# Attention softmax of a fused kernel: mask by a TensorE product, one maximum and one subtraction per group, other order of the first loads

## The chip, the cores and the metric

The kernel runs on one core of a Trainium2 chip. The metric is device time in microseconds for one execution, as a median of repeated runs. A profiled execution is a single one of them, with a trace of every instruction. TensorE is called PE here (its weight loads PEld), VectorE is DVE, ScalarE is ACT, GpSimd is POOL, and SP is the engine whose queue issues the DMA transfers.

## The reference

```python
def _attn_ref(q, k, v):                       # 2 batches, 8 heads, 768 positions, head size 64
    k_sum = k.reshape(B, H, nb, 32, D).max(axis=3)
    v_sum = v.reshape(B, H, nb, 32, D).mean(axis=3)
    scores_l = scale * q @ k.T                # kept where |i - j| < 16, else -1e9
    scores_s = scale * q @ k_sum.T + log(32)
    a = softmax of [scores_l, scores_s], with 1e-9 added to the sum
    return a @ concatenate([v, v_sum])
def reference(...):
    x = attention, as 1536 tokens x 512
    x = (h * cos(h)) @ w_out,  h = x @ w_in           # 512 -> 2048 -> 512
    return layernorm(h * softmax(h)) * g_ln @ w_out2, h = x @ w_in2   # 512 -> 1024 -> 512
```

## The kernel before

Attention takes the first quarter of the time and the two feed-forward layers the rest. Heads go in 8 **pairs** (two heads on 128 partitions), each pair in 3 **groups** of 4 tiles of 64 queries, so there are 24 groups. A loop of 29 **steps** (lines 592 to 658) is a software pipeline: in step s, PE makes the scores of group s+1 (`emit_s`, tile `sps`, one of two PSUM banks), DVE and POOL take mask and maximum of group s (`emit_max`), ACT exponentiates group s-1 (`emit_exp`), DVE sums group s-2 and POOL normalises it (`emit_sum`, `emit_norm`), PE transposes group s-4 (`emit_t`) and multiplies group s-5 by v (`emit_av`). A group's scores are 128 x 480: 4 tiles with a window of 96 keys and 24 block maxima each.

Each pair also has to be prepared. The loads of k and q (`load_heads`, two buffers each) are laid side by side by a copy (`pair_k` on DVE, `pair_q` on ACT, tiles `kg` and `qg`, one buffer each), and PE transposes them in the step after the copies (`emit_k`, `emit_q`); three pairs are in flight. The means of v over blocks come from a second load of v, `vb`, once for each batch: `sum_v` (one DVE reduction for one head of each pair, five POOL additions for the other), `scale_v` on ACT, and `place_vsum`, a DMA that writes them under the window of v in `vt` (three buffers). `sum_v(0)` stands in step 1 and `sum_v(1)` in step 8; the load for the second, `load_vb(1)`, is issued in step 5, into the one `vb` buffer.

The order on every engine is the order in which the code is written: nothing reorders it, and an instruction that waits holds up all behind it in its queue, SP's DMA issues too. PE's row also holds `warm_up` products (two or three in each step before step 15) and from step 15 on the first 48 products `h` of the first feed-forward layer (`FILL`). Between steps 9 and 20 the first weights are converted (`rebias` on ACT, `finish` on DVE, `split` on ACT and POOL), and in steps 7, 10, 13 and 16 a quarter of the attention's output is split into two parts (`split_x`, tile `xs`, ACT and then POOL).

The softmax of one group is, before: four DVE instructions that add the mask from SBUF and take the maximum (line 500), a POOL subtraction (503), the exponential (508), a DVE sum (512), a DVE addition of 1e-9 to the 128x4 sums (516, `emit_guard`), after other DVE work its reciprocal (520), and a POOL product (521).

Of the kernel before, what the change touches and what calls it, by code (L numbers as in the profile page):

```python
# [19 lines left out]
QT = 64  # L20
# [13 lines left out]
def fused_kernel(  # L34
# [56 lines left out]
    wide = w_in.dtype == mybir.dt.int64  # L91
    LOWEST = -3.0e38
    WSTEPS = (9, 10, 12, 13, 15, 17, 18, 19)
# [3 lines left out]
    DVE_X = 19  # L97
    DVE_NORM = 99
    LAST = 5
# [234 lines left out]
    def attention():  # L334
        st = ExitStack()
        with st:
            io = st.enter_context(tc.tile_pool(name="io", bufs=2))
            fix = st.enter_context(tc.tile_pool(name="fix", bufs=1))
            sm_p = st.enter_context(tc.tile_pool(name="sm", bufs=6))

            NM = NG + 2
            mask = fix.tile([P, NM, KW], F32, name="mask")

            q_t, k_t, v_t, kx_t, vs_t, qk_t, ks_t = {}, {}, {}, {}, {}, {}, {}
# [15 lines left out]

            def side_by_side(t, name, scalar):
# [3 lines left out]
                if scalar:  # L365
                    nc.scalar.activation(out=to, in_=t, func=AF.Copy)
                else:
                    nc.vector.tensor_copy(to, t)
                return o

            def pair_k(n):
                k_t[n] = side_by_side(k_t[n], "kg", False)

            def pair_q(n):
                q_t[n] = side_by_side(q_t[n], "qg", True)

# [116 lines left out]

            def emit_max(G):
                g = G % GPP
                sm = sm_p.tile([P, NG, KW], F32, tag="sm", name="sm")
# [8 lines left out]
                sm_t[G] = sm  # L505

            def emit_exp(G):
                nc.scalar.activation(out=sm_t[G], in_=sm_t[G], func=AF.Exp)  # L508

            def emit_sum(G):  # L510
                ss = sm_p.tile([P, NG], F32, tag="ss", name="ss")
                nc.vector.tensor_reduce(out=ss, in_=sm_t[G], op=ALU.add, axis=AX.X)
                sum_t[G] = ss

            def emit_guard(G):
                nc.vector.tensor_scalar_add(sum_t[G], sum_t[G], 1e-9)

            def emit_norm(G):
                sm, ss = sm_t[G], sum_t.pop(G)
                nc.vector.reciprocal(out=ss, in_=ss)  # L520
                (nc.vector if G >= DVE_NORM else nc.gpsimd).tensor_tensor(  # L521
                    out=sm, in0=sm, in1=ss.unsqueeze(2).to_broadcast([P, NG, KW]), op=ALU.mult)

            def emit_t(G):
                sm = sm_t.pop(G)
                aps = bank(2, "aps").rearrange("p (i s) -> p i s", i=NG)[0:KW]
                for i in range(NG):
                    nc.tensor.transpose(aps[:, i, :], sm[:, i, :], ident)
                at_t[G] = aps
# [50 lines left out]
            emit_q(0)  # L580
            emit_kx(0)
            emit_qx(0)
            warm_up(3)
# [8 lines left out]
            for step in range(NGR + LA):  # L592
# [27 lines left out]
                if LT <= step < NGR + LT:  # L620
                    emit_at(step - LT)
                if summed:
                    emit_guard(step - LN)
                weights.finish()
# [297 lines left out]
```

## Time and profile before

| | |
|---|---|
| median of 3 runs | 517.97 us (517.88 to 519.25) |
| the profiled execution | 516.67 us, its span 514.6 us |
| PE busy | 489.6 us, 95% of the span |
| DVE, ACT, POOL busy | 60%, 54%, 30% |
| attention ends, first product `y` of the feed-forward | 117.26 us |

From 117 us on PE is never without work, and none of that part is touched by the change. What the change can give or cost lies in the first 117 us. A line of a timeline gives start, duration, engine, source line and tiles, and in brackets how long the engine stood idle before and what ended that.

### The profile page before, as it was taken

Reading aid. Unit: us, or ns where it says so; the run is one execution under the profiler, and the core shown is the slowest. Engines: PE = TensorE matmul, PEld = TensorE weight load, DVE = VectorE, ACT = ScalarE, POOL = GpSimd, SP = SyncE. Lnnn points to the kernel's source line nnn. Section 1 sums busy time; section 2 is a strip of 40 time slices with the busy share of each in tenths; the row PEclk is TensorE's granted clock in tenths of the full one; section 3 lists DMA queues with packets and bytes.
Section 4 is the critical chain, followed back from the end, with each engine's and each line's share of the span. In section 5 each row is a group of like instructions: output and inputs, shape, how many; then the busy total and the mean of one; then the engine's idle time right before and its main releaser. Section 6 shows DMA issues by size and latency. Waiting matters only on the chain.

```text
span 514.6 us, 7653 instructions
## 1 busy us (share of the span) xinstructions
PE 489.6 (95%) x2855; PEld 395.2 (77%) x2863; DVE 309.7 (60%) x684; ACT 275.4 (54%) x504; POOL 155.9 (30%) x147
## 2 busy tenths in 40 slices
PE   7589798899999999999999999999999999999997
PEld 4366576667888888888888888888887888888887
DVE  2586878786444447466565654646577755665561
ACT  3356798775768666565565653787422223222221
POOL 0477888742422222232232220244103102110000
PEclk8979899999999999999999999999999999999999
DMA  8799995600132322322323321220000000000001
GB/s 250 181 225 194 259 256 141 181 2 1 55 110 82 110 95 82 123 82 91 114 83 97 108 82 41 83 82 2 0 1 21 22 20 22 20 20 22 37 26 41
DMA packets 44516, 44.57 MB, mean 87 GB/s; under 512 B 21440, under 2 KB 36416, under 8 KB 44096
## 3 DMA queue, kind: packets, MB, share of 16 engines
q1 hardware_dynamic: 44480, 44.09, 29.5%
q8 instruction: 22, 0.36, 0.3%
q14 instruction: 14, 0.11, 0.1%
HBM read 39.76 MB, written 3.15 MB: 83 GB/s over the span
## 4 chain that ended last, share of the span: by engine, by line
PE 75%; DVE 6%; DMA 5%; ACT 5%; POOL 4%; SPq 3%; issue 2%; POOLq 0%; DVEq 0%; ACTq 0%
PE y L275 25%; PE h L233 23%; PE o L799 12%; PE h L721 11%; DMA vb<-in_v_dram 4%; PE tp L769 2%; POOL vb L409 1%; POOL sm L521 1%; POOL sm L503 1%; DMA qt<-in_q_dram 1%; SPq L397 1%; DVE vm L405 1%; PE sps L489 1%; POOL w L186 1%; ACT sm L508 1%
## 5 line engine op out<-in xcount | busy, mean ns | idle before, releaser
L233 PE MATMUL h<-xs,w 128*128 128x512 f32 x576 | 141.5, 392 | 1.2 <-ACT qx L475 1.2
L275 PE MATMUL y<-gs,w 128*128 128x512 f32 x576 | 138.2, 389 | 0.0
L275 PEld LDWEIGHTS y<-gs,w 128*128 128x128 f32 x576 | 108.0, 188 | 22.5
L233 PEld LDWEIGHTS h<-xs,w 128*128 128x128 f32 x576 | 107.1, 188 | 23.6 <-ACT qx L475 1.3
L186 POOL TENSOR_TENSOR w<-s,w 128x512 fp32r<-128x512 f32 x48 | 62.1, 1295 | 161.3 <-ACT w L185 139.8
L242 ACT ACTIVATE r<-h 128x512 int32<-128x512 f32 x48 | 28.7, 598 | 86.0 <-PE h L233 86.0
L247 DVE SCALAR_TENSOR_TENSOR r<-r,h 128x512 f32<-128x512 int32 x48 | 32.9, 686 | 67.2 <-ACT r L242 67.0
L799 PE MATMUL o<-w,ls 128*128 128x512 f32 (+1 forms) x312 | 67.8, 374 | 1.4 <-DVE ls L773 1.4
L721 PE MATMUL h<-w,xs 128*128 128x512 f32 x288 | 68.7, 393 | 0.0
L170 DVE SCALAR_TENSOR_TENSOR s<-raw 128x512 int32<-128x512 int32 x48 | 36.4, 757 | 48.3 <-ACT raw L163 40.9
L799 PEld LDWEIGHTS o<-w,ls 128*128 128x128 f32 x312 | 55.3, 188 | 12.2 <-DVE ls L773 1.9
L721 PEld LDWEIGHTS h<-w,xs 128*128 128x128 f32 x288 | 53.3, 188 | 10.7
L738 ACT ACTIVATE e<-h,st 128x1024 f32<-128x1024 f32 (+1 forms) x13 | 13.6, 1050 | 64.3 <-DVE st L734 60.8
L756 POOL TENSOR_TENSOR st<-st,mhalf 128x1 f32<-128x1 f32 x12 | 6.6, 552 | 118.1 <-DVE st L755 105.9
L489 PE MATMUL sps<-kx,qx 64*64 64x120 f32 x384 | 27.5, 288 | 12.1 <-DVE mx L500 12.0
L489 PEld LDWEIGHTS sps<-kx,qx 64*64 64x64 f32 x384 | 21.6, 144 | 22.7 <-DVE mx L500 14.8
L203 POOL TENSOR_TENSOR xs<-X,xs 128x512 fp32r<-128x512 f32 x22 | 28.8, 1314 | 30.7 <-ACT xs L202 30.7
L252 ACT ACTIVATE r<-r,half_pi 128x512 f32<-128x512 f32 x48 | 34.5, 718 | 1.3 <-DVE r L247 1.3
L263 DVE TENSOR_TENSOR gs<-h,gs 128x512 fp32r<-128x512 f32 x48 | 32.6, 679 | 4.1 <-ACT gs L262 3.9
L257 DVE TENSOR_TENSOR h<-h,r 128x512 f32<-128x512 f32 x48 | 32.9, 685 | 0.4 <-ACT r L252 0.4
L162 ACT ACTIVATE raw<-raw 128x512 f32<-128x512 f32 x48 | 32.0, 666 | 0.0
L163 ACT ACTIVATE raw<-raw 128x512 int32<-128x512 uint32 x48 | 31.9, 666 | 0.0
(73 smaller groups left out, 564.3 us busy)
## 6 DMA issues: line engine op xcount, KB each, us to landing
raw<-in_moe_w_in_dram SPq DMA_DIRECT2D x24, 512.0 KB, 3.5
raw<-in_moe_w_out_dram SPq DMA_DIRECT2D x24, 512.0 KB, 3.8
vt<-in_v_dram SPq DMA_DIRECT2D x16, 240.0 KB, 6.4
kt<-in_k_dram SPq DMA_DIRECT2D x8, 384.0 KB, 7.9
qt<-in_q_dram SPq DMA_DIRECT2D x8, 384.0 KB, 6.6
vb<-in_v_dram SPq DMA_DIRECT2D x8, 384.0 KB
out_dram<-osb SPq DMA_DIRECT2D x11, 256.0 KB, 2.0
vt<-vm SPq DMA_DIRECT2D x8, 144.0 KB
```

The lines of the kernel that those rows point to most:

```text
L162: nc.scalar.activation(out=hw, in_=hw, func=AF.Prelu, scale=REBIAS, alpha=NEGATIVE)
L170: nc.vector.scalar_tensor_tensor(out=self.f32[i], in0=t[:, :, 1], scalar=3, in1=t[:, :, 0], op0=ALU.logical_shift_left, op1=ALU.bitwise_or)
L186: nc.gpsimd.tensor_tensor(out=w[:, 1, :], in0=f, in1=as32(w[:, 0, :]), op=ALU.subtract)
L233: nc.tensor.matmul(h, lhsT=w[:, a, f * P:(f + 1) * P], rhs=xs_of[tb, c][:, b_, :], start=(m == 0), stop=(m == 3 * KC - 1))
L247: nc.vector.scalar_tensor_tensor(out=r, in0=r.bitcast(I32), scalar=TWO_PI, in1=h_of[step], op0=ALU.mult, op1=ALU.subtract)
L252: nc.scalar.activation(out=r, in_=r, func=AF.Sin, scale=-1.0, bias=half_pi)
L257: nc.vector.tensor_tensor(out=h, in0=h, in1=r, op=ALU.mult)
L263: nc.vector.tensor_tensor(out=gs[:, 1, :], in0=r, in1=as32(gs[:, 0, :]), op=ALU.subtract)
L275: nc.tensor.matmul(y[e], lhsT=w[:, a, e * P:(e + 1) * P], rhs=gs[:, b_, :], start=(f == 0 and i == 0), stop=(f == GF - 1 and i == 2))
L489: nc.tensor.matmul(sps[h, i, :], lhsT=qx[h, t * QT:(t + 1) * QT], rhs=kx[h, t, :], start=True, stop=True)
L721: nc.tensor.matmul(banks[n], lhsT=xs_of[NTB + t // TPB, c][:, a, t0:t0 + P], rhs=weights.done[w2i[c][n]][:, b_, :], start=(m == 0), stop=( ...
L799: nc.tensor.matmul(o, lhsT=ls_of[t][f // 4][:, a, s0:s0 + P], rhs=w[:, b_, cols], start=(f == 0 and i == 0), stop=(f == NF2 - 1 and i == 2))
```

## The change

- **Mask.** A product of `twice` (the identity plus itself shifted by 64 rows, 128x128) and `maskr` (128x480 of the mask, its upper half rounded, its lower half the remainder) starts each group's PSUM bank; the scores are accumulated on it. `make_mask` builds both tiles once, with two DVE instructions and one on ACT.
- **Maximum.** One DVE reduction over the bank, negated, and one DVE addition of it from PSUM into `sm` replace the four DVE instructions and the POOL subtraction.
- **Guard.** The six `sm` buffers have a 121st column that holds 1e-9, so the sum includes it; `emit_guard` goes, and the reciprocal follows the sum at once.
- **q copies.** From pair 2 on, `pair_q` runs on POOL.
- **Order.** `load_vb(0)` and `load_v(0)` are issued ahead of the loads of pair 2; `sum_v(0)` moves from step 1 to step 3, `scale_v(0)` with the first two `place_vsum` to step 4.

```diff
+            sms = [fix.tile([P, NG, KW + 1], F32, name=f"sm{i}") for i in range(NSM)]
+            for t in sms:
+                nc.gpsimd.memset(t[:, :, KW:KW + 1], 1e-9)
+            def make_mask():
+                half = [ident[:, i * QT:(i + 1) * QT].unsqueeze(1).to_broadcast([P, 2, QT]) for i in range(2)]
+                nc.vector.tensor_tensor(out=twice, in0=half[0], in1=half[1], op=ALU.add)
+                nc.scalar.activation(out=maskr, in_=mask, func=AF.Copy)
+                nc.vector.tensor_tensor(
+                    out=maskr[QT:P], in0=mask[QT:P], in1=as32(maskr[QT:P]), op=ALU.subtract)
...
             def pair_q(n):
-                q_t[n] = side_by_side(q_t[n], "qg", True)
+                q_t[n] = side_by_side(q_t[n], "qg", nc.scalar if n < 2 else nc.gpsimd)
...
+                nc.tensor.matmul(
+                    sps, lhsT=twice.rearrange("p i s -> p (i s)"), rhs=maskr[:, g:g + NG, :],
+                    start=True, stop=False, skip_group_check=True)
                 for i in range(NG):
...
-                            start=True, stop=True)
+                            start=False, stop=True, skip_group_check=True)
...
-                for i in range(NG):
-                    nc.vector.tensor_tensor_reduce(
-                        out=sm[:, i, :], in0=sps[:, i, :], in1=mask[:, g + i, :], scale=1.0, scalar=LOWEST,
-                        op0=ALU.add, op1=ALU.max, accum_out=mx[:, i:i + 1])
-                nc.gpsimd.tensor_tensor(
-                    out=sm, in0=sm, in1=mx.unsqueeze(2).to_broadcast([P, NG, KW]), op=ALU.subtract)
+                nc.vector.tensor_reduce(out=mx, in_=sps, op=ALU.max, axis=AX.X, negate=True)
+                sm = sm_t[G] = sms[G % NSM]
+                nc.vector.tensor_tensor(
+                    out=sm[:, :, 0:KW], in0=sps, in1=mx.unsqueeze(2).to_broadcast([P, NG, KW]), op=ALU.add)
...
                 nc.vector.tensor_reduce(out=ss, in_=sm_t[G], op=ALU.add, axis=AX.X)
+                nc.vector.reciprocal(out=ss, in_=ss)
...
-            def emit_guard(G):
-                nc.vector.tensor_scalar_add(sum_t[G], sum_t[G], 1e-9)
...
+            load_vb(0)
+            load_v(0)
             load_k(2)
             load_q(2)
-            load_vb(0)
-            load_v(0)
...
             emit_kx(0)
+            make_mask()
             emit_qx(0)
...
-                if step == 1:
+                if step == 3:
                     sum_v(0)
-                if step == 2:
+                if step == 4:
                     scale_v(0)
                     place_vsum(0)
+                    place_vsum(1)
...
-                if g == 2 and n + 1 < NPAIR:
+                if g == 2 and 0 < n < NPAIR - 1:
```

**SP, the first loads.** From the second pair's k and q on, before; L350 is a load of k or q, L397 the four transfers of `vb`, L382 and L386 those of `vt`:

```order
L350 DMA kt<-in_k_dram 128x6x128
L350 DMA qt<-in_q_dram 128x6x128
L350 DMA kt<-in_k_dram 128x6x128
L350 DMA qt<-in_q_dram 128x6x128
L397 DMA vb<-in_v_dram 24x2x2048 x4
L382 DMA vt<-in_v_dram 96x10x64
L386 DMA vt<-in_v_dram 96x2x64
L382 DMA vt<-in_v_dram 96x10x64
L386 DMA vt<-in_v_dram 96x2x64
```

The same place on SP after the change:

```order
L362 DMA kt<-in_k_dram 128x6x128
L362 DMA qt<-in_q_dram 128x6x128
L409 DMA vb<-in_v_dram 24x2x2048 x4
L394 DMA vt<-in_v_dram 96x10x64
L398 DMA vt<-in_v_dram 96x2x64
L394 DMA vt<-in_v_dram 96x10x64
L398 DMA vt<-in_v_dram 96x2x64
L362 DMA kt<-in_k_dram 128x6x128
L362 DMA qt<-in_q_dram 128x6x128
```

The third pair's k and q stood ahead of `vb` and `vt`, and stand behind them now.

**POOL, the first steps.** Before, from the first subtractions on (L503 subtraction, L409 and L412 the additions of `sum_v(0)`, L521 normalisation):

```order
L503 TENSOR_TENSOR sm<-sm,mx 128x480 x2
L409 TENSOR_TENSOR vb<-vb 96x1024
L409 TENSOR_TENSOR vb<-vb 96x512
L409 TENSOR_TENSOR vb<-vb 96x256
L409 TENSOR_TENSOR vb<-vb 96x128
L412 TENSOR_TENSOR vm<-vb 96x64
L503 TENSOR_TENSOR sm<-sm,mx 128x480
L521 TENSOR_TENSOR sm<-sm,ss 128x480
```

And after (L380 is the copy of q, L529 the normalisation, L421 and L424 the additions):

```order
L380 COPY qg<-qt 128x2x6x64
L529 ISA
L529 TENSOR_TENSOR sm_97<-sm_97,ss 128x4x120
L529 TENSOR_TENSOR sm_98<-sm_98,ss 128x4x120
L421 TENSOR_TENSOR vb<-vb 96x1024
L421 TENSOR_TENSOR vb<-vb 96x512
L421 TENSOR_TENSOR vb<-vb 96x256
L421 TENSOR_TENSOR vb<-vb 96x128
L424 TENSOR_TENSOR vm<-vb 96x64
L529 TENSOR_TENSOR sm_99<-sm_99,ss 128x4x120
L380 COPY qg<-qt 128x2x6x64
```

The copy of the third pair's q and two normalisations now stand ahead of the additions.

**POOL, a step with an output split.** Before, step 10, where L203 is POOL's half of `split_x` and L186 its half of a weight split:

```order
L521 TENSOR_TENSOR sm<-sm,ss 128x480
L203 TENSOR_TENSOR xs<-X,xs 128x512
L186 TENSOR_TENSOR w<-s,w 128x512
L503 TENSOR_TENSOR sm<-sm,mx 128x480
L521 TENSOR_TENSOR sm<-sm,ss 128x480
L186 TENSOR_TENSOR w<-s,w 128x512
L503 TENSOR_TENSOR sm<-sm,mx 128x480
```

The same step after:

```order
L529 TENSOR_TENSOR sm_99<-sm_99,ss 128x4x120
L201 TENSOR_TENSOR xs<-X,xs 128x512
L380 COPY qg<-qt 128x2x6x64
L184 TENSOR_TENSOR w<-s,w 128x512
L529 TENSOR_TENSOR sm_100<-sm_100,ss 128x4x120
L184 TENSOR_TENSOR w<-s,w 128x512
L529 TENSOR_TENSOR sm_101<-sm_101,ss 128x4x120
```

The subtractions are gone, and the copy of q stands right behind the output split; steps 7, 13 and 16 have the same order.

## Rows read from the trace of the kernel before

**Rows 1.** The page's first part: busy us, share of the span, instructions.

```profile
PE 489.6 (95%) x2855; PEld 395.2 (77%) x2863; DVE 309.7 (60%) x684; ACT 275.4 (54%) x504; POOL 155.9 (30%) x147
```

**Rows 2.** Stretches: length, busy PE, PEld, DVE, ACT, POOL, clock, DMA share, GB/s.

```profile
60.00:80.00 20.00, 19.25 (x250) 14.40 (x248) 16.12 (x71) 18.55 (x38) 17.93 (x17) 1.00 0.76 207
80.00:100.00 20.00, 17.21 (x211) 13.06 (x210) 15.09 (x58) 16.78 (x34) 14.96 (x15) 1.00 0.72 180
100.00:117.00 17.00, 15.32 (x176) 11.26 (x176) 15.68 (x52) 11.20 (x21) 9.13 (x11) 1.00 0.10 33
```

**Rows 3.** The chain that ended last, in order of time: start, us, what.

```profile
9.95 12.05 DMA vb<-in_v_dram
...
27.96 0.94 SPq L423
...
38.28 10.70 DMA vb<-in_v_dram
...
101.40 0.99 POOL sm L503
...
122.93 2.72 PE h L233 x12
```

**Rows 4.** SP's issues, 21 to 39 us: start, us, queue, line, transfer.

```profile
21.94 0.96 SPq L350 DMA_DIRECT2D kt<-in_k_dram  x1
...
29.79 0.55 SPq L350 DMA_DIRECT2D kt<-in_k_dram  x1
...
31.41 0.54 SPq L382 DMA_DIRECT2D vt<-in_v_dram  x1
...
35.83 2.82 SPq L397 DMA_DIRECT2D vb<-in_v_dram  x4
```

**Rows 5.** A stretch of 4 us in the first loads, columns as in the second group.

```profile
8.00:12.00 4.00, 4.00 (x27) 2.54 (x26) 1.49 (x3) 1.64 (x4) 0.00 (x0) 0.58 1.10 331
```

**Rows 6.** POOL's timeline, the additions of the first block means.

```profile
22.16 5.03 POOL L409 TENSOR_TENSOR vb<-vb 96x1024 f32<-96x1024 f32 x4 [5.09 <-DMA vb<-in_v_dram]
```

**Rows 7.** DVE's timeline, its reductions for the block means.

```profile
22.12 3.63 DVE L405 TENSOR_REDUCE vm<-vb 96x64 f32<-96x2048 f32 x1 [5.90 <-DMA vb<-in_v_dram]
...
49.17 3.68 DVE L405 TENSOR_REDUCE vm<-vb 96x64 f32<-96x2048 f32 x1 [3.39 <-DMA vb<-in_v_dram]
```

**Rows 8.** PE's timeline from 72 us, steps 14 and 15.

```profile
72.11 0.88 PE L431 MATMUL qk<-ident,kg 128*128 128x128 f32 x6
72.82 0.82 PE L431 MATMUL qk<-ident,qg 128*128 128x128 f32 x6
73.39 0.95 PE L233 MATMUL h<-xs,w 128*128 128x512 f32 x3
74.27 1.04 PE L489 MATMUL sps<-kx,qx 64*64 64x120 f32 x16
```

**Rows 9.** ACT's timeline, step 13.

```profile
70.91 0.67 ACT L202 ACTIVATE xs<-X 128x512 fp32r<-128x512 f32 x1
71.44 0.88 ACT L366 ACTIVATE qg<-qt 128x768 f32<-128x768 f32 x1
```

**Rows 10.** POOL's timeline, step 13.

```profile
71.27 1.15 POOL L521 TENSOR_TENSOR sm<-sm,ss 128x480 f32<-128x480 f32 x1 [2.08 <-DVE ss L520]
72.37 1.28 POOL L203 TENSOR_TENSOR xs<-X,xs 128x512 fp32r<-128x512 f32 x1
```

**Rows 11.** Instructions by line, 0 to 120 us: count | busy us, mean ns | idle before.

```profile
L503 POOL TENSOR_TENSOR sm<-sm,mx 128x480 f32<-128x480 f32 x24 | 24.9, 1039 | 17.9 <-DVE mx L500 14.0 <-DVE ss L516 4.0
...
L500 DVE CUSTOM_DVE_ANT_0 sm<-sps,mask 128x120 f32<-128x120 f32 x96 | 21.0, 275 | 0.0
...
L512 DVE TENSOR_REDUCE ss<-sm 128x4 f32<-128x480 f32 x24 | 15.1, 629 | 0.7 <-ACT sm L508 0.7
...
L516 DVE TENSOR_SCALAR ss<-ss 128x4 f32<-128x4 f32 x24 | 12.9, 536 | 0.0
...
L186 POOL TENSOR_TENSOR w<-s,w 128x512 fp32r<-128x512 f32 x8 | 10.3, 1283 | 1.6 <-ACT w L185 1.6
...
L257 DVE TENSOR_TENSOR h<-h,r 128x512 f32<-128x512 f32 x3 | 2.1, 689 | 0.0
```

More of the change, by code (lines that the diff above doesn't have):

```diff
@@ L91, in fused_kernel @@
     wide = w_in.dtype == mybir.dt.int64
-    LOWEST = -3.0e38
     WSTEPS = (9, 10, 12, 13, 15, 17, 18, 19)
@@ L97, in fused_kernel @@
     DVE_X = 19
-    DVE_NORM = 99
     LAST = 5
@@ L339, in attention @@
             sm_p = st.enter_context(tc.tile_pool(name="sm", bufs=6))
+            NSM = 6
+            sms = [fix.tile([P, NG, KW + 1], F32, name=f"sm{i}") for i in range(NSM)]
+            for t in sms:
+                nc.gpsimd.memset(t[:, :, KW:KW + 1], 1e-9)
             NM = NG + 2
             mask = fix.tile([P, NM, KW], F32, name="mask")
+            maskr = fix.tile([P, NM, KW], F32R, name="maskr")
+            twice = fix.tile([P, 2, QT], F32R, name="twice")
+            def make_mask():
[4 more added lines that the diff above has]
+                    out=maskr[QT:P], in0=mask[QT:P], in1=as32(maskr[QT:P]), op=ALU.subtract)
             q_t, k_t, v_t, kx_t, vs_t, qk_t, ks_t = {}, {}, {}, {}, {}, {}, {}
@@ L359, in load_k, with side_by_side @@
                 k_t[n] = load_heads(k, n, "kt")
-            def side_by_side(t, name, scalar):
+            def side_by_side(t, name, engine):
                 o = io.tile([P, S // P, 2, D], F32, tag=name, name=name, bufs=1)
                 to = o.rearrange("p c h d -> p h c d")
-                if scalar:
+                if engine is nc.scalar:
                     nc.scalar.activation(out=to, in_=t, func=AF.Copy)
                 else:
-                    nc.vector.tensor_copy(to, t)
+                    engine.tensor_copy(to, t)
                 return o
             def pair_k(n):
-                k_t[n] = side_by_side(k_t[n], "kg", False)
+                k_t[n] = side_by_side(k_t[n], "kg", nc.vector)
             def pair_q(n):
-                q_t[n] = side_by_side(q_t[n], "qg", True)
+                q_t[n] = side_by_side(q_t[n], "qg", nc.scalar if n < 2 else nc.gpsimd)
             def load_v(n):
@@ L490, in emit_s @@
                             sps[h, i, :], lhsT=qx[h, t * QT:(t + 1) * QT], rhs=kx[h, t, :],
-                            start=True, stop=True)
+                            start=False, stop=True, skip_group_check=True)
                 ss_t[G] = sps
             def emit_max(G):
-                g = G % GPP
-                sm = sm_p.tile([P, NG, KW], F32, tag="sm", name="sm")
                 sps = ss_t.pop(G)
                 mx = sm_p.tile([P, NG], F32, tag="mx", name="mx")
-                for i in range(NG):
-                    nc.vector.tensor_tensor_reduce(
-                        out=sm[:, i, :], in0=sps[:, i, :], in1=mask[:, g + i, :], scale=1.0, scalar=LOWEST,
-                        op0=ALU.add, op1=ALU.max, accum_out=mx[:, i:i + 1])
-                nc.gpsimd.tensor_tensor(
-                    out=sm, in0=sm, in1=mx.unsqueeze(2).to_broadcast([P, NG, KW]), op=ALU.subtract)
-                sm_t[G] = sm
+                nc.vector.tensor_reduce(out=mx, in_=sps, op=ALU.max, axis=AX.X, negate=True)
+                sm = sm_t[G] = sms[G % NSM]
+                nc.vector.tensor_tensor(
+                    out=sm[:, :, 0:KW], in0=sps, in1=mx.unsqueeze(2).to_broadcast([P, NG, KW]), op=ALU.add)
             def emit_exp(G):
-                nc.scalar.activation(out=sm_t[G], in_=sm_t[G], func=AF.Exp)
+                sm = sm_t[G][:, :, 0:KW]
+                nc.scalar.activation(out=sm, in_=sm, func=AF.Exp)
             def emit_sum(G):
@@ L512, in emit_sum @@
                 nc.vector.tensor_reduce(out=ss, in_=sm_t[G], op=ALU.add, axis=AX.X)
+                nc.vector.reciprocal(out=ss, in_=ss)
                 sum_t[G] = ss
-            def emit_guard(G):
-                nc.vector.tensor_scalar_add(sum_t[G], sum_t[G], 1e-9)
             def emit_norm(G):
[L519 to L522, printed above, removed]
+                sm = sm_t[G][:, :, 0:KW]
+                nc.gpsimd.tensor_tensor(
+                    out=sm, in0=sm, in1=sum_t.pop(G).unsqueeze(2).to_broadcast([P, NG, KW]), op=ALU.mult)
             def emit_t(G):
@@ L527, in emit_t @@
                 for i in range(NG):
-                    nc.tensor.transpose(aps[:, i, :], sm[:, i, :], ident)
+                    nc.tensor.transpose(aps[:, i, :], sm[:, i, 0:KW], ident)
                 at_t[G] = aps
@@ L621, in attention @@
                     emit_at(step - LT)
-                if summed:
-                    emit_guard(step - LN)
                 weights.finish()
```

## The prediction

> **What bounds the kernel now.** I read the busy shares first: PE is busy 95% of the span [rows 1], and from 122 us on the chain of waits is PE alone, 12 products in 2.72 us, one after the other [rows 3]. Nothing of that part changes, so the change is worth what it does before 117 us. There the chain has two halves. Up to 49 us it is the second load of v: `vb(0)` lands at 22.00 (9.95 + 12.05), POOL adds its blocks, SP can then issue `place_vsum` at 27.96, the transfers in between follow, `vb(1)` is issued from 35.83 on and its last part lands at 48.98 [rows 3, 4]. DVE shows the same as two waits, 5.90 us before the first reduction and 3.39 us before the second [rows 7]. From 55 us on every engine is nearly full, and the fullest is PE: 19.25 of 20 us from 60 to 80, 17.21 of 20 from 80 to 100, 15.32 of 17 after that [rows 2]. So PE stands idle 0.75 + 2.79 + 1.68 = 5.2 us from 60 to 117 us. DVE has 3.9 us to spare in the first of these stretches, POOL 2.1, ACT 1.5.
>
> **What is taken away, and what it is worth.** POOL loses 24 subtractions of 1.04 us, 24.9 us. DVE loses 96 masked maxima (21.0 us) and 24 guards of 0.54 us (12.9 us), and gets 24 reductions at 0.63 us (the row of the sum, also 128x480) and 24 additions at 0.69 us (the row of a product with one input in PSUM, 128x512): 31.7 us for 33.9 [rows 11]. ACT loses six q copies of 0.88 us [rows 9]. All this is work beside PE. It shortens the way from scores to exponential by one POOL instruction, and that can give back only what PE now idles.
>
> **First half: plus 2.5 us.** In the first loads, `vb(0)` and `vt(0)` move ahead of the third pair's k and q. Those are 0.79 MB, at 331 GB/s [rows 5] 2.4 us, so both land that much earlier, and `vb(0)` is there at 19.6. But `sum_v(0)` no longer starts when it lands. On POOL it now stands behind the copy of the third q and two normalisations. SP got past `vt(0)` at 21.94 [rows 4]; less 2.4 us, it issues the third k at 19.5 and the third q about 1 us later, behind all the bytes of `vt(0)`, and the q should be there near 24.4, as long as the sum of the bytes is the same. The wait of DVE moves with it: `pair_k(2)` waits for the k, where `sum_v(0)` waited for `vb`, to about 23 us against 22.12 [rows 7]. On POOL: 24.4, copy 1.0, two normalisations of about 1 us (0.99, as the subtraction over the same tile [rows 3]), so the additions start at 27.4 against 22.16, take the same 5.03 us [rows 6] and 0.3 for the last of them and for ACT, and `place_vsum(0)` can be issued near 33.1 against 27.96: 5.2 us later. SP's next transfers are queued behind that wait. The loads of the fifth pair, 29.79 to 31.41 before, now stand ahead of it, which gives 1.6 us back [rows 4]. So `vb(1)` is issued 3.5 us later, near 39.4. It took 13.1 us from there to land and shared the queues with later loads, of which less will be under way then; I take 2.5 us for its landing, near 51.5. Bounds: plus 1.0 (the q there at 23, a short copy, an emptier queue) and plus 4.5. Nothing covers it: DVE waited 3.39 us for this very load [rows 7], and so arrives in time either way. The mask tiles, the memsets and the two more DVE instructions at the start, some 3 us before the first group, lie in the 5.90 us that DVE waited anyway [rows 7]: nothing.
>
> **Second half, the mask products: plus 3.2 us.** PE gets one product of 480 columns for each group. A product of 512 columns takes 2.72 / 12 = 0.227 us in a row of its like [rows 3], and three of them in the loop take 0.88 (73.39 to 74.27), 0.29 each [rows 8]; so 0.21 to 0.27 each for 480. Groups 10 to 23 come after the wait for `vb(1)`: 14 products, 3.0 to 3.8 us, in a row that is 96% full. I take 3.2, near the lower end, as the weights of all but the first product of a group were loaded beside others already. The ten groups before lie beside the waits for loads.
>
> **Second half, q copies: plus 2.0 us.** The copy was on ACT, right behind ACT's half of the output split: 70.91 and 71.44, done at 72.32, and PE took up q at 72.82, half a microsecond later and without a wait [rows 8, 9]. On POOL it stands behind POOL's half of that split, which needs ACT's half (done at 71.58) and takes 1.28 us [rows 10]. Its normalisation ahead comes sooner than now, as the reciprocal no longer waits behind other DVE work (2.08 us in rows 10), so the split starts near 71.6, ends at 72.9, and the copy ends near 73.9: PE could go on at 73.95 instead of 72.82, 1.1 us later. Behind q in PE's row stand the h products, the next scores, the next transposes. This comes three times after 54 us, for pairs 5, 6 and 7; 3.3 us in all, of which I count 2.0, since a wait here takes the place of small waits for ACT in the same three steps. The price of the copy is not in the trace. ACT's 0.88 us for the same tile [rows 9] is the lower bound; POOL's 1.28 us for 512 elements from two inputs [rows 11], scaled to 768, makes 1.9 the upper. I take 1.0, nearer the first, as it has one input. That gives 0 to 4.5 us for this term. The Trainium skill, page "GPSIMD Engine Reference", section 4.1 "Engine selection", says that operations with one input run at roughly line rate there; with the 1.2 GHz of its specifications an estimate is 0.64 us for 768 elements, and the sum by that would be 3.0 us in place of 4.0.
>
> **Second half, what comes back: minus 3.7 us.** Of PE's 3.5 idle us from 60 to 100 I give back 3.2: they are waits for ACT and DVE, which have less to do, while PE has more. Behind 100 us, where the subtraction and the normalisation of each step follow each other on POOL (101.40 is such a subtraction [rows 3]) and PE idles 1.68 us [rows 2], I count 0.5; the rest is the last groups' way through the sine and its products, which loses little more than three guards.
>
> **Sum.** 2.5 + 3.2 + 2.0 - 3.7 = 4.0 us on the profiled execution's 516.67 (span 514.6 and 2.07 around it): 520.7. The median of the runs, 517.97, is 1.3 above that execution, and the forecast is given on it: 522.0.
>
> **Rivals.** *Faster: the path was the softmax, not PE.* A busy PE is not one at its peak, so its 96% may be rows that stretch while they wait for others. If the mask product fits beside weight loads and the q copy comes before PE asks for it, then both plus terms of the second half are gone and all of the 5.2 idle us [rows 2] come back: 2.5 - 5.2 = -2.7, 515.3. For it speaks that a guard over 128x4 elements takes 0.54 us on average, hardly less than a sum over 480 [rows 11]: something holds it up. The Trainium skill, page "GPSIMD Engine Reference", section 1 "Specifications", says that POOL's interface to SBUF is shared with VectorE, in contention with DVE's modes on two ports or with two SBUF inputs; by that rule the guards wait for POOL, and the time would be this rival's. Against it speaks that DVE idles 3.9 of 20 us as it is [rows 2].
>
> *No change: the first half costs little.* If `vb(1)` lands only 1 us later, and PE's returns and costs in the second half nearly cancel (3.0 + 1.0 - 4.5), the sum is 0.5: 518.5.
>
> *Much slower: the copy is dear.* At 1.9 us the copy delays the first half by 0.9 us more and PE's waits by 0.9 us three times: 4.0 + 0.9 + 2.7 = 7.6, 525.6. It decides from about 1.5 us a copy. The copies of k on DVE run at the same time from the same loads, which may lengthen both.
>
> *The change does not do what it says.* Reduction and addition could be longer than their rows, each working from PSUM on a four-tile pattern. At 0.2 us more a group, DVE's 3.9 spare us in 20 would still hold it; the sum stays at 4.
>
> **How the numbers follow.** Forecast (with the fourth rival): 0.50; much slower: 0.13; no change: 0.17; faster: 0.20. I take 522.0. A measurement tells about 0.3%, 1.55 us, from no change: slower has 0.63, the same 0.17, faster 0.20. The range goes from 515.0, just under the faster rival's time (which leaves half of that case out), to 526.5, past the dear copy; the forecast's own, with its bounds added as far as they are independent, is 519 to 525.
>
> **What would show it.** Right: `sum_v(0)` on POOL starts near 27 us and the second DVE reduction near 52; after that PE shows a mask row of 0.21 to 0.29 us in each group, waits of about 1 us before q with POOL's copy as releaser, and y starts near 121. Wrong: POOL's additions start before 25 us (the loads came earlier than I count); the copy takes 0.7 us or less and PE never waits for it; PE's idle time between 60 and 100 us stays or grows with other releasers; or y starts before 117 us (the softmax was the path).

## The result, and the profile after the change

| | before | after |
|---|---|---|
| median of 11 runs each | 517.88 us | 522.20 us |
| lowest and highest | 516.29, 519.25 | 520.07, 524.42 |
| profiled execution, its span | 516.67, 514.6 | 520.2, 518.4 |
| first product `y` of the feed-forward | 117.26 | 120.67 |

After / before is 1.0089, with a 95% interval of 1.0066 to 1.0111: 4.3 us by the medians, 4.6 by the ratio, slower. The prediction was 522.0.

The page's first part (busy us, share of the span, instructions) moved as the diff says: POOL lost 19 us, PE gained 9, DVE kept its time with 166 instructions fewer [rows 1].

```profile
PE 498.6 (96%) x2879; PEld 401.8 (78%) x2887; DVE 311.5 (60%) x518; ACT 272.1 (52%) x499; POOL 136.8 (26%) x135
```

**The first half.** The chain of waits of after, in order of time (start, us, what):

```profile
27.49 0.99 POOL sm L529
28.48 2.34 POOL vb L421
...
41.49 10.70 DMA vb<-in_v_dram
52.37 3.74 DVE vm L417
...
87.91 0.78 POOL qg L380
88.73 0.88 PE qk L443 x6
...
120.67 5.68 PE y L273 x24
```

Before, the additions followed the landing of `vb(0)` at 22.00 [rows 3]. Now they follow a normalisation on POOL. `vb(1)` has the same 10.70 us on the chain as before, 3.2 us later. POOL's timeline (start, duration, engine, line, operation, in brackets the idle time ahead and what ended it) shows what POOL's row waited for, the third pair's q:

```profile
25.68 0.82 POOL L380 COPY qg<-qt 128x768 f32<-128x768 f32 x1 [24.62 <-DMA qt<-in_q_dram]
26.55 1.93 POOL L529 TENSOR_TENSOR sm<-sm,ss 128x480 f32<-128x480 f32 x2
28.44 5.08 POOL L421 TENSOR_TENSOR vb<-vb 96x1024 f32<-96x1024 f32 x4
```

DVE's timeline at its second reduction, and SP's issues (start, us, queue, line, transfer) of the third pair's q, of `place_vsum` and of `vb(1)`:

```profile
52.37 3.74 DVE L417 TENSOR_REDUCE vm<-vb 96x64 f32<-96x2048 f32 x1 [2.58 <-DMA vb<-in_v_dram]
```

```profile
20.17 1.70 SPq L362 DMA_DIRECT2D qt<-in_q_dram  x1
...
34.29 1.77 SPq L435 DMA_DIRECT2D vt<-vm  x2
...
39.77 2.08 SPq L409 DMA_DIRECT2D vb<-in_v_dram  x4
```

Against [rows 4, 6, 7]: the additions start at 28.44 (22.16 before), `place_vsum` is issued at 34.29 (27.96), `vb(1)` at 39.77 (35.83), and DVE's second reduction starts at 52.37 (49.17). The last is 3.2 us, and `y` is 3.4 us later: in this execution nearly all of the difference is there at 52 us already. From the first `y` to the end of the span it is 397.7 us after and 397.3 before. That part is not PE alone, as the prediction has it: the chain of before runs through DVE and ACT from 379.90 to 398.98. But it is alike in both kernels.

**The second half.** From DVE's second reduction to the first `y` it is 68.30 us after (120.67 - 52.37) and 68.09 before. Three stretches of after that end at 120.4 (length, busy PE, PEld, DVE, ACT, POOL, clock, DMA share, GB/s), as [rows 2] end at 117:

```profile
63.40:83.40 20.00, 19.28 (x230) 14.23 (x229) 17.01 (x30) 16.70 (x35) 15.04 (x14) 1.00 0.76 203
83.40:103.40 20.00, 18.99 (x231) 14.11 (x230) 14.49 (x26) 16.81 (x35) 10.39 (x11) 1.00 0.70 179
103.40:120.40 17.00, 16.24 (x183) 12.19 (x181) 14.86 (x30) 11.15 (x21) 5.82 (x7) 1.00 0.10 34
```

PE idles 0.72 + 1.01 + 0.76 = 2.5 us of 57, where it idled 5.2. The two lengths of 68 us can't be compared as they stand, though, since the granted clock differs just ahead of these stretches. PE's first work behind DVE's second reduction, before:

```profile
55.14 1.36 PE L489 MATMUL sps<-kx,qx 64*64 64x120 f32 x16 [4.52 <-DVE mx L500]
56.43 1.11 PE L528 MATMUL aps<-ident,sm 128*120 128x128 f32 x4
```

```profile
56.00:60.00 4.00, 3.89 (x36) 2.49 (x35) 2.94 (x14) 4.00 (x8) 2.94 (x4) 0.61 1.02 325
```

And after:

```profile
59.12 0.49 PE L497 MATMUL sps<-maskr,twice 128*128 128x480 f32 x1 [3.13 <-DVE sm L514]
59.53 1.04 PE L504 MATMUL sps<-kx,qx 64*64 64x120 f32 x16
60.50 0.65 PE L536 MATMUL aps<-ident,sm 128*120 128x128 f32 x4
```

Before, PE had stood idle for 4.52 us, and the clock granted from 56 to 60 us was 0.61, which is a mean of the full level (2.4 GHz) and the half one (1.2 GHz). The same 16 score products and four transposes took 1.36 and 1.11 us there, and 1.04 and 0.65 after, where PE had idled 3.13 us and the clock stayed at 1.00. With the products by v and the `warm_up` products that follow, this is some 1.5 us (an estimate from these rows). So the second half of after is some 1.7 us longer than that of before without this stretch, and has been spared about as much of slower products. The prediction has no term for the clock.

PE's timeline shows every wait for POOL's copy of q after the change:

```profile
26.56 1.29 PE L443 MATMUL qk<-ident,qg 128*128 128x128 f32 x6 [1.59 <-POOL qg L380]
77.09 0.87 PE L443 MATMUL qk<-ident,qg 128*128 128x128 f32 x6 [0.61 <-POOL qg L380]
88.73 0.88 PE L443 MATMUL qk<-ident,qg 128*128 128x128 f32 x6 [0.17 <-POOL qg L380]
```

Two of them lie behind 54 us, 0.8 us in all, and the last copy is on the chain above (87.91). The mask product on the chain, at one of its places (start, us, what):

```profile
62.52 0.21 PE sps L497
```

In the running row it is 0.21 to 0.24 us on the chain; at the two places where PE had just waited for DVE it is 0.49 and 0.48 (59.12 and 100.86). The groups of after by line (count, busy us and mean ns of one, idle before):

```profile
L380 POOL COPY qg<-qt 128x768 f32<-128x768 f32 x6 | 5.0, 825 | 24.6 <-DMA qt<-in_q_dram 24.6
```

```profile
L514 DVE TENSOR_TENSOR sm<-sps,mx 128x480 f32<-128x480 f32 x24 | 15.8, 658 | 2.1
L523 DVE TENSOR_REDUCE ss<-sm 128x4 f32<-128x484 f32 x24 | 15.5, 647 | 1.3 <-ACT sm L519 1.3
L512 DVE TENSOR_REDUCE mx<-sps 128x4 f32<-128x480 f32 x24 | 15.2, 634 | 0.0
```

Maximum and addition from PSUM cost 0.634 and 0.658 us, as the prediction took them (0.63 and 0.69), and the guard column makes the sum 0.02 us longer.

### The profile page after: what moved, and what is told of

Its sections match the earlier page's. It is cut to its first block, busy times and chain, and to the rows that moved or that the text cites. A ratio compares the mean times of both kernels' runs of the same rounds, so it can differ in the third digit from the quotient of the medians.

```text
span 518.4 us, 7507 instructions
## 1 busy us (share of the span) xinstructions
PE 498.6 (96%) x2879; PEld 401.8 (78%) x2887; DVE 311.5 (60%) x518; ACT 272.1 (52%) x499; POOL 136.8 (26%) x135
## 4 chain that ended last, share of the span: by engine, by line
PE 78%; DVE 7%; ACT 4%; DMA 4%; POOL 2%; issue 2%; SPq 2%; DVEq 0%; POOLq 0%; ACTq 0%
PE y L273 25%; PE h L231 24%; PE o L807 12%; PE h L729 11%; DMA vb<-in_v_dram 2%; PE tp L777 2%; DMA qt<-in_q_dram 2%; PE sps L504 1%; PE qk L443 1%; POOL vb L421 1%; PE aps L536 1%; ACT kx L464 1%; PE ops L554 1%; DVE vm L417 1%; DVE s L168 1%
## 5 line engine op out<-in xcount | busy, mean ns | idle before, releaser
L168 DVE SCALAR_TENSOR_TENSOR s<-raw 128x512 int32<-128x512 int32 x48 | 37.7, 785 | 45.9 <-ACT raw L161 39.2
L183 ACT ACTIVATE w<-s 128x512 fp32r<-128x512 f32 x48 | 30.1, 628 | 3.3 <-DVE s L168 3.0
L260 ACT ACTIVATE gs<-h 128x512 fp32r<-128x512 f32 x48 | 28.1, 586 | 2.8 <-DVE h L255 2.8
```

Of the source, the lines that this page charges most:

```text
L168: nc.vector.scalar_tensor_tensor(out=self.f32[i], in0=t[:, :, 1], scalar=3, in1=t[:, :, 0], op0=ALU.logical_shift_left, op1=ALU.bitwise_or)
```

## Experiments

All ratios are to the kernel before on the same chip, with a 95% interval; two changed kernels are compared by their ratios, since they ran on three chips. One per cent is 5.2 us.

### The order alone, and all but the order

The kernel before with the new order of loads and of `sum_v(0)`:

```diff
-            load_k(2)
-            load_q(2)
             load_vb(0)
             load_v(0)
+            load_k(2)
+            load_q(2)
...
-                if step == 1:
+                if step == 3:
                     sum_v(0)
-                if step == 2:
+                if step == 4:
                     scale_v(0)
                     place_vsum(0)
+                    place_vsum(1)
...
-                if g == 2 and n + 1 < NPAIR:
+                if g == 2 and 0 < n < NPAIR - 1:
```

> The kernel before with only the new order of the first loads and of the first block sums. Theory A (the new order puts POOL's first additions behind other POOL work, SP's queue and the second block load follow): POOL here still has its subtractions, so the additions wait for four softmax instructions and start near 29 us, the second load of v lands near 54 us instead of 49.0, and the time is 4 to 5 us over the kernel before. Theory B (the order is neutral, the mask product on PE makes the loss): within 1 us of the kernel before.

Measured: 524.41 us, 1.0122 (1.0092 to 1.0152), 6.3 us, more than theory A's 4 to 5. The opposite edit on the changed kernel:

> The changed kernel with the order of first loads and block sums of the kernel before. Theory A: the second load of v lands at 49 us again (52.2 in the changed kernel), and 3.2 us of the 4.3 us loss go: 0.5 to 1.5 us over the kernel before. Theory B: the loss stays, 4 us over the kernel before.

Measured: 519.15 us, 1.0023 (1.0007 to 1.0039). So the order costs 1.0089 - 1.0023, 3.4 us (known to 1.4) in the changed kernel, and 6.3 us (known to 1.5) on the kernel before. Not all of the latter need be the late load: the mean granted clock of these six executions was 0.976 to 0.984, that of the kernel before beside them 0.980 to 0.987. POOL's additions and DVE's second reduction show the order's part. Order alone:

```profile
31.10 5.24 POOL L409 TENSOR_TENSOR vb<-vb 96x1024 f32<-96x1024 f32 x4
```

```profile
55.35 3.74 DVE L405 TENSOR_REDUCE vm<-vb 96x64 f32<-96x2048 f32 x1 [1.34 <-DMA vb<-in_v_dram]
```

The changed kernel with the old order:

```profile
21.59 5.05 POOL L421 TENSOR_TENSOR vb<-vb 96x1024 f32<-96x1024 f32 x4 [5.25 <-DMA vb<-in_v_dram]
```

```profile
49.58 3.74 DVE L417 TENSOR_REDUCE vm<-vb 96x64 f32<-96x2048 f32 x1 [2.80 <-DMA vb<-in_v_dram]
```

With the old order both are back at 22 and 49 us. On the kernel before, POOL's row ahead of the additions still holds its subtractions of 0.99 us, which wait for DVE, so they start 2.7 us later than in the changed kernel (31.10 against 28.44).

### Is it the order of the loads, or what stands ahead of the additions?

Two kernels keep the loads of `vb(0)` and `vt(0)` ahead of the third pair, but write `sum_v(0)` in step 1 ahead of the copies of k and q; the changed kernel so, and the kernel before so:

```diff
+                if step == 1:
+                    sum_v(0)
                 if g == 1 and n + 2 < NPAIR:
                     pair_k(n + 2)
                     pair_q(n + 2)
...
```

The line of `sum_v(0)` in its former place goes, and in the changed kernel `scale_v(0)` and the first two `place_vsum` return to their steps of before.

> The changed kernel with its new order of loads, but the first block sums stand in step 1, ahead of the copies of the third pair's k and q, and the first two placements in step 2. Theory A (it is the POOL work ahead of the additions, not the order of the loads, that makes the second load of v late): the additions start when the load lands, near 19.5 us instead of 28.4, the first placement is issued near 25 us instead of 34.3, the second load of v lands at 46 to 48 us instead of 52.2, and the time is 4 to 5 us under the changed kernel, 0 to 1 us under the kernel before. Rival E (the new order of loads is itself what costs): 521 us or more.

> The kernel before with the new order of loads and the first block sums in step 1 ahead of the copies of the third pair. Theory A: its additions start near 19.5 us instead of 22.2 and the second load of v lands 1 to 2 us earlier than 49.0; 1 to 2 us under the kernel before, unless the third q, now late on ACT, holds up the exponentials, which would take the gain back (0). Rival E (the order of loads costs in itself): 3 us or more over the kernel before.

Measured: 519.38 us, 1.0027 (1.0007 to 1.0048) on the changed kernel, and 518.16 us, 0.9999 (0.9979 to 1.0019) on the kernel before. So the order of the loads alone does no harm that can be seen, and what stands ahead of the additions (with the place of the `place_vsum` that follow them) does. But the earlier landing of `vb(0)`, near 19.2 us as predicted (19.6), gains nothing. In the changed kernel so altered the additions start at 19.24, and SP issues (start, us, transfer):

```profile
25.34 1.15 SPq L398 DMA_DIRECT2D vt<-in_v_dram  x1
26.59 1.78 SPq L435 DMA_DIRECT2D vt<-vm  x2
...
35.39 2.50 SPq L409 DMA_DIRECT2D vb<-in_v_dram  x4
```

The means were ready at 25, SP was still issuing `vt(1)`, and `vb(1)` goes out at 35.39, where it went out before (35.83). SP's own issues are late next. I had expected 4 to 5 us under the changed kernel from the first run and got 3.2, and 1 to 2 us under the kernel before from the second, which gained nothing (in its profiled execution, the slowest of its twelve, `vb(1)` went out at 37.69).

### The q copies, in the changed kernel and alone

On the changed kernel, with `pair_q` back on ACT; and with the old order as well, so that only mask, maximum and guard are left of the change:

```diff
-                q_t[n] = side_by_side(q_t[n], "qg", nc.scalar if n < 2 else nc.gpsimd)
+                q_t[n] = side_by_side(q_t[n], "qg", nc.scalar)
```

> The changed kernel with the q copies on ACT again. Theory A: POOL's first additions start 0.8 us earlier, which the second load of v keeps, and the three waits of PE for q after 60 us (0.8 us in all) go; 1 to 2 us less than the changed kernel, 2.5 to 3.5 us over the kernel before. Theory C (the copies on POOL make most of the loss): 0 to 1 us over the kernel before. Theory D (ACT is as full as PE, and the copies on POOL save time): slower than the changed kernel by 1 us or more.

> Old order, q copies on ACT: only the mask product, the single maximum and subtraction and the guard column are left of the change. Theory A: the 3 us that the 14 mask products cost PE after 55 us and the idle time of PE that comes back cancel: within 1 us of the kernel before. Theory B (mask products are the loss): 3 us over. Rival (the softmax was the path): 2 us or more under the kernel before.

Measured: 521.66 us, 1.0068 (1.0044 to 1.0093) with the new order, and 519.29 us, 1.0020 (0.9998 to 1.0042) with the old one. With the old order the copies on POOL cost nothing that can be seen (1.0023 against 1.0020, known to 1.4 us). With the new one they may cost 1 us; the intervals overlap. In the profiled execution with the new order and the copies on ACT the additions even start at 30.91, but 1.8 us of that is the third q, which came later: ACT's copy starts at 27.50, POOL's in the changed kernel at 25.68. From there to the additions it is 3.41 us, and 2.76 in the changed kernel, so the copy on ACT, with exponentials waiting behind it, saves nothing there. (The expectation counts three waits behind 60 us; the rows above show two.) Then the copies alone, on the kernel before:

```diff
-                q_t[n] = side_by_side(q_t[n], "qg", True)
+                q_t[n] = side_by_side(q_t[n], "qg", True if n < 2 else nc.gpsimd)
```

> The kernel before with one edit: from pair 2 on the copy of q runs on GpSimd. The prediction counted 2.0 us for this in the second half (three waits of PE for q of about 1.1 us); by it the time is 2 us or more over before, ratio 1.004 to 1.008, the more as POOL here still has its 24 subtractions. Theory A as it stands after the first runs (the copy takes 0.82 us and PE waits for it 0.8 us in all): ratio 0.999 to 1.002. Rival (the copy only costs nothing since the subtractions are gone from POOL's row): PE's waits with this copy as releaser add up to over 2 us here, and the ratio is 1.004 or more.

Measured: 519.89 us, 1.0041 (1.0015 to 1.0068), 2.1 us. The rival held by its waits; the interval of the time just reaches theory A's. The same copy of 0.82 us is late here; PE's two waits, and POOL's row ahead of the first:

```profile
74.01 0.87 PE L433 MATMUL qk<-ident,qg 128*128 128x128 f32 x6 [1.49 <-POOL qg L366]
86.14 0.87 PE L433 MATMUL qk<-ident,qg 128*128 128x128 f32 x6 [1.47 <-POOL qg L366]
```

```profile
68.52 0.98 POOL L505 TENSOR_TENSOR sm<-sm,mx 128x480 f32<-128x480 f32 x1
70.81 1.15 POOL L523 TENSOR_TENSOR sm<-sm,ss 128x480 f32<-128x480 f32 x1 [1.30 <-DVE ss L522]
71.92 1.27 POOL L203 TENSOR_TENSOR xs<-X,xs 128x512 fp32r<-128x512 f32 x1
73.14 0.82 POOL L366 COPY qg<-qt 128x768 f32<-128x768 f32 x1
```

PE goes on at 74.01, where the prediction had 73.95, but not by its working: the prediction let POOL's half of the split start right behind ACT's, and here it starts 0.80 us behind it (ACT's half ends at 71.12), since the normalisation ahead still waits for DVE. ACT's half comes earlier than in the prediction's row (71.58 there) and the copy is shorter, and the three cancel. In the changed kernel the same place reads, on POOL:

```profile
74.98 1.28 POOL L201 TENSOR_TENSOR xs<-X,xs 128x512 fp32r<-128x512 f32 x1 [3.22 <-ACT xs L200]
76.22 0.82 POOL L380 COPY qg<-qt 128x768 f32<-128x768 f32 x1
```

There POOL stands idle for 3.22 us until ACT's half of the split comes, the copy follows as here, and PE waits 0.61 us. Counted from the end of ACT's half (74.90 there, 71.12 here), POOL's half starts 0.08 us behind it in place of 0.80, and PE asks for q 1.58 us behind it in place of 1.40. At the second place (86.56 and 83.26) it is 0.07 in place of 0.79, and 2.00 in place of 1.41. So 0.72 us of each wait went with the free row of POOL, and 0.2 and 0.6 us because PE comes later; why it does, no run shows.

### The mask product, left out and done twice

```diff
-                nc.tensor.matmul(
-                    sps, lhsT=twice.rearrange("p i s -> p (i s)"), rhs=maskr[:, g:g + NG, :],
-                    start=True, stop=False, skip_group_check=True)
```

> The changed kernel without the product that adds the mask (the mask and the log of the block size are left out of the scores; all else stays). Theory A (PE sets the pace after 55 us): 14 products of 0.21 to 0.27 us go from a full row, 3 us under the changed kernel (519). Rival F (the way from scores to exponential sets the pace, PE's row only stretches): within 1 us of the changed kernel.

```diff
                 nc.tensor.matmul(
                     sps, lhsT=twice.rearrange("p i s -> p (i s)"), rhs=maskr[:, g:g + NG, :],
                     start=True, stop=False, skip_group_check=True)
+                nc.tensor.matmul(
+                    sps, lhsT=twice.rearrange("p i s -> p (i s)"), rhs=maskr[:, g:g + NG, :],
+                    start=True, stop=False, skip_group_check=True)
```

> The changed kernel with the mask product issued twice for each group, the second over the first. Theory A: 14 more products of 0.21 us in PE's full row, 3 us over the changed kernel (525). Rival F: within 1 us of it.

Measured: 520.9 us, 1.0063 (1.0038 to 1.0088) without it, and 524.25 us, 1.0126 (1.0096 to 1.0155) with two. Against the changed kernel that is 1.3 us less and 1.9 us more, where 3 was expected each time. Each of these is known only to 1.7 and 1.9 us, so neither alone is clear of nothing. Between none and two products, on one chip, lie 3.3 us, known to 2.0: 0.6 to 2.6 us a set. That is below theory A's 3, and rival F's 1 us is not excluded. Of the last 57 us ahead of `y` these are the first 40, without the product, and with two (columns as above):

```profile
66.10:86.10 20.00, 18.89 (x233) 13.69 (x233) 15.97 (x28) 16.85 (x35) 14.70 (x13) 1.00 0.73 197
86.10:106.10 20.00, 17.98 (x234) 13.50 (x230) 14.84 (x27) 17.03 (x35) 10.65 (x10) 1.00 0.72 176
```

```profile
67.80:87.80 20.00, 19.82 (x233) 14.84 (x232) 15.98 (x26) 15.87 (x33) 13.86 (x13) 1.00 0.62 174
87.80:107.80 20.00, 19.54 (x233) 14.67 (x234) 14.31 (x26) 16.69 (x34) 10.44 (x10) 1.00 0.66 164
```

In these 40 us PE idles 3.1 us without the product, 1.7 with one (the first two stretches of after), 0.6 with two. So with each set of products 1.1 to 1.4 us of idle time go. An estimate of 14 products of 0.21 us less that is 1.5 to 1.8 us a set, in keeping with the times. The granted clock again stands beside this: from DVE's second reduction to `y` it is 68.54 us without the product, 68.30 with one and 71.82 with two, but the first and the last execution went at 0.50 from 60 to 64 us, and the changed kernel at 1.00. The two that went alike differ by 3.3 us, 1.6 a set. Over all executions the mean clock was 0.981 without the product, 0.987 with one and 0.989 with two; whether the product itself keeps the clock up, six executions don't show.

### The second load of v sooner

If the landing of `vb(1)` sets the first half, issuing it sooner should gain. On the kernel before, and on the changed kernel with the old order:

```diff
+                if step == 4:
+                    load_vb(1)
                 if g == 1 and n + 1 < NPAIR:
                     load_v(n + 1)
...
-                if step == 5:
-                    load_vb(1)
```

> The kernel before with one edit: the second load of v (vb of batch 1) is issued in step 4 behind the loads of the fifth pair's k and q and ahead of vt(2), in place of step 5. Theory A (up to 49 us the path runs through this load, so its issue time sets the time): it is issued near 31.4 us instead of 35.8, lands 3 to 4 us earlier, near 45, DVE's wait ahead of its second reduction (3.39 us before) falls under 1 us, and the time is 2 to 3.4 us under before, ratio 0.993 to 0.996. Rival B (the queues are full of bytes there, and what is issued sooner shares them and lands no sooner, or makes vt(2) late): same time within 1 us, ratio 0.998 to 1.002, and the load lands within 1 us of 48.98. Rival C (PE's row, not this load, is the limit of the first half): the load lands sooner, DVE's wait goes, and the time is the same.

> The changed kernel with the order of the first loads and of sum_v(0) as before, and with the second load of v in step 4, as in the run on the kernel before. Theory A: the same gain as there, 2 to 3.4 us under the changed kernel with the old order (ratio 1.0023), so ratio 0.995 to 0.999. Rival B: 1.000 to 1.004, unchanged.

And on the latter in step 2, right behind `place_vsum(0)`:

```diff
                 if step == 2:
                     scale_v(0)
                     place_vsum(0)
+                    load_vb(1)
...
-                if step == 5:
-                    load_vb(1)
```

> The changed kernel with the old order, and the second load of v issued in step 2, right behind place_vsum(0), where its buffer comes free. Theory A: issued near 29 us, ahead of all the loads of the fifth pair and of vt(2); it lands near 41 to 43, DVE's wait for it is gone, and what is late next is the fifth pair's k and q, which are needed some 10 us later; ratio 0.992 to 0.998. Rival B (the 1.5 MB ahead of them make the next pair's k, q and vt late, and PE waits for those): 1.002 to 1.010.

Measured: 517.04 us, 0.9988 (0.9962 to 1.0013); 517.39 us, 0.9994 (0.9968 to 1.0019); 517.07 us, 0.9990 (0.9968 to 1.0013). The wait goes; on the kernel before so altered, DVE starts at once:

```profile
47.83 3.76 DVE L405 TENSOR_REDUCE vm<-vb 96x64 f32<-96x2048 f32 x1
```

But of DVE's wait (3.39 us before, 2.80 with the old order) only 0.6 us comes back on the kernel before, less than the interval, and 1.5 and 1.7 on the changed one, known to 1.6 and 1.4. On the kernel before this is what rival C foretold, though not by PE's row: what is late next stands on the chain of that kernel:

```profile
39.53 7.92 SPq L386
...
54.61 3.80 DMA raw<-in_moe_w_in_dram
```

An issue for `vt(2)`, now behind `vb(1)`, holds SP for 7.92 us, and the first weights of the feed-forward, which SP issues after that (at 54.61, before at 52.04), take over the chain, as they do in the other two kernels. Whether those weights, issued from elsewhere, would let the gain through was not tried. None of these kernels is shown to beat the kernel before.

## Why the forecast held, and which of its terms did not

The sum of plus 4.0 us came out as 4.3 to 4.6. By the experiments the halves held too: plus 2.5 and plus 1.5 were predicted, 3.4 us (the order, known to 1.4) and 1.2 us (1.0023, the rest, known to 0.8) were measured. But that the number came within 0.2 us (522.0 and 522.20) is luck: the first half was 0.9 us too small and the second 0.3 too large, less than either is known to; inside the second half two large terms were both too large and cancelled, and one, the copies, can't be seen. The profiled executions split otherwise: 3.2 us up to the second reduction and 0.2 us after it, where products at the full clock gave back some 1.5 us.

- **First half, 2.5 us: the mechanism was right, the size a little small.** The q landed near 25.7 and not 24.4, so the additions started at 28.44 (27.4 predicted); the queue gave 2.4 us of that back (1.6 were assumed), and `vb(1)` was issued at 39.77 (39.4). DVE came to it at 52.37 (51.5). 3.4 us lies within the bounds of 1.0 to 4.5. That nothing covers it left out PE's clock (above). The mask tiles cost nothing with the old order: the changed kernel's additions start at 21.59 there, no later than before. For the new order this is not shown, since the chain of after does run through ACT's `maskr` (9.37, 0.70 us) on its way to SP's issues at 21.06.
- **q copies, 2.0 us: wrong for the changed kernel.** The copy takes 0.82 us, below the 0.88 that I had as its lower end: one input of 768 elements is no dearer on POOL than on ACT. But the size was not the main step that failed. The working let POOL's row change (the split starts 0.08 us behind ACT's half, as it has it), but took PE's time of asking from the row of before: 72.82 - 71.58, 1.24 us behind ACT's half, and PE asked 1.58 and 2.00 behind it. So the waits were 0.61 and 0.17 us in place of 1.1, and for the third pair that it counted there was none. The time shows nothing of them (1.0023 against 1.0020). On the kernel before, where POOL's row does not change, they are 1.49 and 1.47 us, and the time is 2.1 us longer. The Trainium skill, page "GPSIMD Engine Reference", section 4.1 "Engine selection", has one-input operations at roughly line rate; by that the prediction had an estimate of 0.64 us. The trace has 0.82, which is 0.18 over it and as much under the 1.0 that I took.
- **Mask products, 3.2 us, and what comes back, 3.7 us: both too large.** A product does take 0.21 us in PE's running row (62.52 on the chain), as predicted. But I charged all of them in full and gave the idle time back in full. The products lie partly in that idle time: 0.6 to 2.6 us was their cost, near 1.6, and idle time of 2.7 us went (5.2 to 2.5), 1.1 to 1.4 of it filled by them. Mask, maximum and guard together came to plus 1.0 us (interval -0.1 to 2.2); the prediction's two terms together, to minus 0.5. With 1.6 us for the products the return was some 0.6 us (an estimate, no better known than these two) and not 3.7.
- **Rivals.** *Faster, the softmax path:* fell; with the old order and the old copies the new softmax is not faster (1.0020). What spoke for it was real, though: guards were long beside POOL's work (last section), and all 24 are gone, without a gain. *No change* comes near the changed kernel with the old order, 519.15. *Much slower:* fell with a copy of 0.82 us. *Longer instructions on DVE:* 0.634 and 0.658 us, not longer.
- **Parts do not add up.** Order, q copies and softmax cost 6.3, 2.1 and 1.0 us, each alone on the kernel before: 9.4 in all, and 4.6 together. Both the order and the copies put work on POOL's row or behind it, and the softmax part takes 24 subtractions out of that row, and the late reciprocal: for the copies the rows show this as 0.72 us at each of two places. For the order it is argued, and the lower clock of that run stands beside it.

Of the signs that the prediction named, three were right (additions near 27, second reduction near 52, `y` near 121), one held in part (the mask row, 0.21 to 0.24 us in a running row and 0.48 behind a wait), and one was wrong (waits of about 1 us before q). It would have been wrong if PE's idle time from 60 to 100 us had stayed; that shrank, but without the time coming back, and so proves no return.

## What to carry to other kernels

Before an addition of work is charged in full and an idle stretch given back in full, ask whether the one will lie in the other: here both terms were too large. A moved step costs what stands ahead of it in the queue of its new place, so cost it on the queue as the whole change leaves it, and undo single parts from the changed kernel as well as adding them to the old one: here the order cost 6.3 us on the old kernel and 3.4 in the changed one, the copies 2.1 and nothing that could be seen. Before two stretches of two executions are compared, read the granted clock of each, from the wait ahead of them on. When a load on the chain is issued sooner, look at what its issue pushes back in the issuing queue, since that is the next to be late.

## What the hardware showed that was not expected

- **POOL's copy equals ACT's.** 128x768 fp32 into a two-part pattern takes 0.82 us on POOL and 0.83 to 0.90 on ACT, while POOL's two-input row of 128x512 takes 1.28 [rows 11].
- **DVE instructions are long beside POOL's.** Rows of after, DVE and then POOL:

```profile
73.66 0.69 DVE L168 SCALAR_TENSOR_TENSOR s<-raw 128x512 int32<-128x512 int32 x1 [1.75 <-ACT raw L161]
...
77.12 1.70 DVE L168 SCALAR_TENSOR_TENSOR s<-raw 128x512 int32<-128x512 int32 x1 [0.21 <-POOL qg L380]
```

```profile
77.00 1.28 POOL L184 TENSOR_TENSOR w<-s,w 128x512 fp32r<-128x512 f32 x1
78.24 1.43 POOL L529 TENSOR_TENSOR sm<-sm,ss 128x480 f32<-128x480 f32 x1
```

  The DVE instruction takes 0.69 us at 73.66, where POOL is idle. At 77.12 it ends 0.54 us behind POOL's product, and POOL's next, 0.99 us by itself, takes 1.43. The guard of before, 128x4 elements, took 0.16 us at 55.00, where POOL was idle; at 65.55, beside a POOL product, it took 0.83 and ended with it, at 66.4:

```profile
65.55 0.83 DVE L516 TENSOR_SCALAR ss<-ss 128x4 f32<-128x4 f32 x1
```

```profile
65.09 1.27 POOL L186 TENSOR_TENSOR w<-s,w 128x512 fp32r<-128x512 f32 x1
```

  The Trainium skill, page "GPSIMD Engine Reference", section 1 "Specifications", says that POOL's interfaces to SBUF are shared with VectorE, in contention with DVE instructions in a two-port mode or with two SBUF inputs. These rows agree with a shared interface, and in the guard's row the price of a short instruction is the rest of POOL's; which of the two conditions holds for which instruction they don't show.
- **An issue on SP can take 8 us.** A load that elsewhere in the same run takes 0.9 to 1.4 us to issue (L386) held SP's queue for 7.92 us (39.53, above), with the 1.5 MB of `vb(1)` just ahead of it, and one held it for 5.82 us at 43.78 before. What stands behind it in SP's order is issued later by as much.
- **The same kernel's first loads land at different times.** DVE's first reduction, which waits for `vb(0)`, started at 22.12 in the profiled execution of before and at 24.61 with `vb(1)` sooner, where nothing ahead of it differs. Single profiles can't be compared to better than some 2 us in this first half; the medians decide.
- **The clock differs between executions of one kernel.** Of 35 executions of the kernel before on one chip, the four with a mean granted clock of 0.990 took 515.7 us on average, the twelve near 0.987 517.4, the sixteen near 0.983 518.1, and the three at 0.980 520.4. In the profiled execution of before (mean 0.987) it was 0.61 behind PE's wait of 4.52 us.
